# Interleaved banded groups in the second batch, with sums of v and half of the masks taken off the tensor engine, and 70 unread matmuls

## The chip, the core and the metric

The kernel runs on one core of a Trainium2 chip. The metric is device time in microseconds (us) of one execution. In the texts PE is the tensor engine (matmuls and transposes), DVE the vector engine, ACT the scalar engine, POOL the GpSimd engine and SP the engine that issues the DMAs.

## What is computed

The reference takes q, k and v of 8 batches x 8 heads x 576 tokens x 64 and sums two attentions per head: one on tokens that are averaged in fours (144 tokens, "pooled"), whose result is repeated four times, and one in which a token sees only the 7 tokens around it (the "band"). The result, as 4608 tokens x 512, goes through a layer that takes the maximum of three products, and then through an output product:

```python
pos = np.arange(S)
mask = np.abs(pos[:, None] - pos[None, :]) < factor
scores = scale * np.matmul(q, k.transpose(0, 1, 3, 2))
scores = np.where(mask, scores, -1000000000.0)
...
return (out_up + out_local).astype(np.float32)

def _moe_ref(x, w1, w2, w3, w_out) -> np.ndarray:
    h = np.maximum(np.maximum(x @ w1, x @ w2), x @ w3)
    return (h @ w_out).astype(np.float32)
```

In the program's inputs the weights are float64 (their 64 bits are read as two 32-bit words), and the products of the layer are made from a high and a low part of each operand: three matmuls (high x high, high x low, low x high) for each product.

## The kernel before

**Tiles and stages.** A batch has 512 tokens in 128 rows of four, and 64 tokens of tail; the tails of all batches make a ninth block. Half a batch (4 heads) is a group, n = 0 to 17; groups 2j and 2j+1 make batch j. For each batch `mlp_in` runs 216 matmuls of 128x512 (6 slices of the hidden layer x 3 weights x 4 slices of x x 3 parts) and `mlp_out` 72, so 2592 in nine blocks. `transposes(j, c)` adds the pooled result `od` to the band result `x` and splits the sum into `xhi` and `xlo` (ACT casts, DVE or POOL subtracts), which the layer's matmuls read.

**Two ways to do the band.** Groups 0 to 3 (`DENSE`) compute the band on PE: `band_load` loads, `band_transposes` (T) brings q and k to feature-major form, `band_scores` for each of two head pairs (A, B) makes 128x134 pieces of scores with an additive mask that a matmul `identr` x `maskr` writes to the PSUM bank first, then a maximum (DVE), an exponential (ACT) and a scaling (POOL or ACT). `band_values` (V, W) transposes the probabilities and multiplies them with v. Groups 4 to 17 do it on DVE, ACT and POOL (`scores`, `values`), with products of 128x1792 elements on DVE. The pooled attention is made by `tail_pooled` (t), `pooled_scores` (p), `band_pooled_values` (v: the sums of four rows of v, by matmuls of 128x256 with a matrix `sums` of zeros and ones) and `pooled_values` (o).

**Weights.** `weight_in` and `weight_out` turn 64-bit words into a float32 high and low part: an absolute value on ACT, a clamp (`tensor_scalar` with max and min, on DVE or POOL by `WENG`), three bit operations on DVE, a cast on ACT, a subtraction. In the profile the work tile is `wo` (`wa`), and the results are `whi` and `wlo`. The tags `whi2`, `whi3`, `whi4`, `whi5` (and `wlo`) serve groups 0 to 3 first as homes of scores and transposed q and k.

**What sets the order.** Nothing is issued as it is written. A `Recorder` takes down every operation with its tiles, then `place()` deals them to the engines by a list: each operation has a price per engine (`price`), a priority and the operations that it needs; the engine that is free first takes the ready operation with the lowest key (time, priority, order of writing). What may go to several engines goes to the one that ends first by these prices. A tile can be opened only when a buffer of its tag is free and it is among the next `WINDOW` tiles of its tag. The order of each engine is fixed by this before the program runs; on the chip an engine issues in that order and waits wherever an operand is not there. PE and the others are thus in order, and so is SP with the DMAs. PSUM has eight banks in two tags of four, `pm` and `pa`; the layer's matmuls use `pm`, the attention `pa`, and group 0 uses `pm` as well.

The first batch is written in the order of the string `ORDER`, groups 0 and 1 interleaved, at priority 0. The second batch is `block(1)`: `attention(2)` at priority 200, and after it `attention(3)` at 300. PE work has 2000 taken off its priority, and `mlp_in`, `mlp_out` stand at -100.

All instructions go through one line of `emit` (L374 in the profile), so the groups of the profile are told apart by their tiles.

```python
ORDER = "T0 T1 A0 A1 B0 V0 B1 V1 t0 p0 t1 p1 W0 W1 v0 o0 v1 o1"
PE_MASK = (0, 1, 2, 3)
WINDOW = {"pa": 4, "pm": 4}
```

## Time and profile before

| | |
|---|---|
| Median of 3 runs | 822.71 us (818.24 to 826.49) |
| The profiled execution's own time | 821.14 us |
| Its span | 819.4 us, 12160 instructions |
| Mean granted clock of PE | 0.975 |
| PE busy | 787.8 us (96%), 4064 matmuls |
| DVE busy | 660.5 us (81%) |
| ACT busy | 422.2 us (52%) |
| POOL busy | 361.6 us (44%) |
| Mean share of the DMA engines | 94 GB/s, 76.72 MB |

A row of the windows view gives a stretch in us from the span's start, its length, and then for each engine its busy time and its instructions, then the granted clock of PE as a share of the full one, the DMA share and GB/s. A row of the timeline gives start, duration, engine, line, operation, output and inputs, shapes and count, and in brackets the idle time ahead of it and what ended it. Matmuls overlap, so what one costs is read from the distance between two starts and not from its duration. A float32 matmul appears as two instructions in the profile, and as one in the order of the program; transposes, and matmuls of the rounded type (names that end in `r`), appear as one in both. The tile names are those of the tag: `xhi`, `whi`, `wo`, `pv`, `hh` carry several tenants in turn, so `whi<-pm,mxb` in the first 80 us is an exponential of scores.

### The profile page before, as it was taken

The page shows a single profiled execution, that of the slowest core. Times are in us where ns is not written, and L with a number is a line of the kernel's source. Part 1 is how long each engine was busy: PE and PEld are TensorE (multiplying, and loading weights), DVE is VectorE, ACT ScalarE, POOL GpSimd, SP SyncE. Part 2 cuts the span into 40 slices and gives each one's busy share as a digit, 9 for nine tenths or more (in the row PEclk, how much of TensorE's full clock was granted, in tenths as well). Part 3 has the DMA queues.
Part 4 walks back from the last instruction along what each step waited for, and adds up shares of the span by engine and source line. Part 5 has one row for each costly group of instructions (what it writes and reads, how often), then busy time and mean ns, then how long its engine had stood idle before and what let it go on. Part 6 is the DMA issues. An engine that isn't in the chain of part 4 may idle for free.

```text
span 819.4 us, 12160 instructions
## 1 busy us (share of the span) xinstructions
PE 787.8 (96%) x4064; PEld 609.9 (74%) x4064; DVE 660.5 (81%) x859; ACT 422.2 (52%) x1446; POOL 361.6 (44%) x522
## 2 busy tenths in 40 slices
PE   6879999999999999999899999999899999999997
PEld 4657776777777777777677777778677887888885
DVE  5999668799999999999999999999999962231220
ACT  7867657435583737567274746726483451121111
POOL 0642101136878847697477956768162341000000
PEclk9668999999999999999999999999999999999999
DMA  7754033334323423352234334422242210001002
GB/s 243 186 174 118 10 103 110 110 102 131 108 97 107 125 77 90 102 157 84 84 110 135 110 88 113 143 85 88 77 133 73 79 58 26 1 13 39 1 0 52
DMA packets 63177, 76.72 MB, mean 94 GB/s; under 512 B 21484, under 2 KB 43434, under 8 KB 63114
## 3 DMA queue, kind: packets, MB, share of 16 engines
q1 hardware_dynamic: 63114, 75.94, 30.8%
q8 instruction: 32, 0.52, 0.3%
q14 instruction: 31, 0.25, 0.1%
HBM read 66.49 MB, written 9.44 MB: 93 GB/s over the span
## 4 chain that ended last, share of the span: by engine, by line
PE 64%; DVE 20%; ACT 6%; issue 5%; DMA 2%; POOL 2%; POOLq 0%; SPq 0%; DVEq 0%; ACTq 0%
PE pm L374 52%; PE pa L374 11%; DVE prod L374 4%; DVE s L374 3%; DVE x L374 3%; ACT pv L374 2%; POOL pv L374 2%; DVE wo L374 1%; DMA v<-in_v_dram 1%; ACT wlo L374 1%; DVE y L374 1%; DVE pm L374 1%; DVE t L374 1%; DMA pv<-in_k_dram 1%; DVE xlo_0r L374 1%
## 5 line engine op out<-in xcount | busy, mean ns | idle before, releaser
L374 PE MATMUL pm<-xhi_0r,whi_0r 128*128 128x512 f32 x648 | 258.4, 399 | 0.0
L374 PE MATMUL pm<-xhi_0r,wlo_0r 128*128 128x512 f32 x648 | 258.3, 399 | 0.0
L374 PE MATMUL pm<-xlo_0r,whi_0r 128*128 128x512 f32 x648 | 258.2, 399 | 0.0
L374 POOL TENSOR_TENSOR pv<-v,s 128x256 f32<-128x256 f32 x247 | 177.6, 835 | 93.7 <-DVE s L374 72.1
L374 ACT ACTIVATE pv<-v,s 128x64 f32<-128x64 f32 x580 | 151.7, 412 | 21.8 <-DMA v<-in_v_dram 9.8
L374 PEld LDWEIGHTS pm<-xhi_0r,whi_0r 128*128 128x128 f32 x648 | 122.4, 189 | 28.3 <-issue 0.2
L374 PEld LDWEIGHTS pm<-xlo_0r,whi_0r 128*128 128x128 f32 x648 | 122.2, 189 | 28.1 <-issue 0.4
L374 PEld LDWEIGHTS pm<-xhi_0r,wlo_0r 128*128 128x128 f32 x648 | 122.1, 188 | 27.8
L374 DVE TENSOR_TENSOR prod<-k,q 128x1792 f32<-128x1792 f32 x56 | 119.2, 2128 | 1.1 <-DMA k<-in_k_dram 0.9
L374 DVE TENSOR_REDUCE x<-pv 128x256 f32<-128x1792 f32 x55 | 110.2, 2006 | 7.2 <-POOL pv L374 7.1
L374 DVE TENSOR_REDUCE s<-prod 128x28 f32<-128x1792 f32 x56 | 112.4, 2007 | 0.4
L374 DVE TENSOR_TENSOR t<-pm,t 128x512 f32<-128x512 f32 x54 | 36.9, 683 | 63.9 <-PE pm L374 63.8
L374 PE MATMUL pm<-wo_1r,hh_0r 128*128 128x512 f32 x216 | 85.6, 397 | 0.0
L374 PE MATMUL pm<-wo_1r,hh_1r 128*128 128x512 f32 x216 | 85.4, 399 | 0.0
L374 DVE TENSOR_TENSOR pm<-pm,t 128x512 f32<-128x512 f32 x54 | 37.3, 691 | 25.1 <-PE pm L374 24.9
L374 ACT CAST hh_1r<-pm 128x512 fp32r<-128x512 f32 x30 | 17.6, 588 | 71.3 <-DVE pm L374 71.3
L374 ACT COPY t<-pm 128x512 f32<-128x512 f32 x54 | 31.8, 589 | 40.0 <-PE pm L374 39.9
L374 ACT CAST hh_0r<-pm 128x512 fp32r<-128x512 f32 x24 | 14.1, 588 | 67.8 <-DVE pm L374 67.5
L374 PEld LDWEIGHTS pm<-wo_1r,hh_1r 128*128 128x128 f32 x216 | 41.0, 190 | 10.0 <-issue 0.5
L374 ACT COPY y<-pm 128x512 f32<-128x512 f32 x38 | 22.2, 588 | 49.6 <-PE pm L374 42.3
L374 PE MATMUL pm<-wo_0r,hh_1r 128*128 128x512 f32 x120 | 47.5, 400 | 0.1
L374 PEld LDWEIGHTS pm<-wo_1r,hh_0r 128*128 128x128 f32 x216 | 40.9, 189 | 9.1
(262 smaller groups left out, 1142.6 us busy)
## 6 DMA issues: line engine op xcount, KB each, us to landing
v<-in_v_dram SPq DMA_DIRECT2D x55, 320.0 KB
k<-in_k_dram SPq DMA_DIRECT2D x55, 320.0 KB
out_dram<-y SPq DMA_DIRECT2D x36, 256.0 KB
q<-in_q_dram SPq DMA_DIRECT2D x56, 128.0 KB
hh<-in_moe_w_dram SPq DMA_DIRECT2D x12, 512.0 KB
pv<-in_moe_w_dram SPq DMA_DIRECT2D x6, 512.0 KB
pv<-in_moe_w_out_dram SPq DMA_DIRECT2D x6, 512.0 KB
wo<-in_v_dram SPq DMA_DIRECT2D x12, 128.0 KB
```

The costliest lines, as they stand in the source:

```text
L374: getattr(self.engines[o.eng], method)(*map(real, args), **{k: real(x) for k, x in kw.items()})
```

## The change

1. **Second batch interleaved.** `second_block` takes the place of `block(1)`: groups 2 and 3 are written in the order of a new string `ORDER2`, both at priority 200, through the same table of steps (`steps_of`) as the first batch. Group 3 gets the separate buffers that group 1 had (`OTHER = (1, 3)`), so the two groups don't share them.
2. **Masks.** `PE_MASK` goes from four groups to groups 0 and 1. In groups 2 and 3 the 16 mask matmuls go; DVE adds the mask to each bank of scores and writes the sum to SBUF (`sm`), where the maximum and the exponential read it.
3. **Sums of v.** `band_pooled_values` no longer uses matmuls: for each head it loads 128x256 of v once more, and DVE or POOL add the halves (128x128 per head), then the halves of the halves (128x256 per group). The matrix `sums`, its load and its tile go.
4. **Unread matmuls.** `WARM` goes from 0 to 70: 70 matmuls `identr` x `identr` of 128x512 into one `pm` bank that nobody reads, at priority 1e6, so that `place()` puts one wherever PE has nothing else ready by its reckoning.
5. **Transposes of groups 0 and 1** write their output with a step of four elements into the PSUM bank (`inorder`), so that the copy out of it reads and writes in a row. Before, PE wrote in a row and ACT read with a step.
6. **Loads of the tails** of k and v in groups 0 and 1 use the two buffers of tag `q` in place of the one of `traw`.
7. **Prices and windows.** `place()` reckons a `tensor_scalar` on POOL with 4.1 ns an element in place of 2.2, and `WINDOW` is 3 in place of 4 for both PSUM tags. `GATE` is empty and does nothing.

```diff
-WARM = 0
+WARM = 70
-PE_MASK = (0, 1, 2, 3)
+PE_MASK = (0, 1)
+OTHER = (1, 3)
+ORDER2 = "L2 T2 L3 A2 B2 V2 W2 T3 t2 p2 A3 B3 v2 o2 V3 W3 t3 p3 v3 o3"
-WINDOW = {"pa": 4, "pm": 4}
+WINDOW = {"pa": 3, "pm": 3}
...
+            if method == "tensor_scalar":
+                return 140.0 + 4.1 * n, True
             return 140.0 + (1.68 if kw.get("op") == ALU.mult else 2.2) * n, True
...
-            raw = new([N64, FAC * D], tag="traw", name=f"traw_{n}_{g}")
+            raw = new([N64, FAC * D], tag="q", bufs=2, name=f"traw_{n}_{g}") if n < 2 and g else new([N64, FAC * D], tag="traw", name=f"traw_{n}_{g}")
...
+                    inorder = ps.rearrange("p (r f) -> p f r", f=FAC)
                     for f in range(FAC):
-                        pe.transpose(ps[:, P * f : P * f + P], byf[:, f], ident)
-                    to, fr = dst.rearrange("p (r f) -> p f r", f=FAC), ps.rearrange("p (f r) -> p f r", f=FAC)
+                        pe.transpose(inorder[:, f], byf[:, f], ident)
+                    to, fr = dst, ps
...
-            for i in range(2):
+            for i in range(2) if on_pe else ():
                 pe.matmul(sps[i], identr, rest, start=True, stop=False, skip_group_check=True)
-                banks[tp, i] = sps[i]
...
+            for i in range(2):
+                banks[tp, i] = sps[i]
+                if not on_pe:
+                    dve.tensor_tensor(out=sm[:, i, 2 * tp : 2 * tp + 2], in0=sps[i], in1=rest.bitcast(F32), op=ALU.add)
+                    banks[tp, i] = sm[:, i, 2 * tp : 2 * tp + 2]
...
-        ps = bank([P, HH, D], tag, f"psv_{n}")
-        for u in range(FAC):
-            pe.matmul(ps, sums[:, 96 - 32 * u : 96 - 32 * u + P], vt[:, u], start=u == 0, stop=False, skip_group_check=True)
-        pe.matmul(ps[96:], sums[:6, 64:96], vb[1][:, 1], start=False, stop=True, tile_position=(0, 96), skip_group_check=True)
-        copy(vd, ps)
+        hv = new([P, HH, 2 * D], tag="hv", name=f"hv_{n}")
+        vd = state[n]["vd"] = new([P, HH, D], tag="vd", bufs=2, name=f"vd_{n}")
+        for g in range(HH):
+            vv = new([P, FAC * D], tag="v", bufs=2, name=f"v_{n}_{g}")
+            sp.dma_start(vv, row_tokens(v, j, h0 + g, 0, FAC * D))
+            halves(n, "v", vv, hv[:, g], BENG)
+        tt(vd, hv[:, :, :D], hv[:, :, D:], ALU.add, BENG)
...
+    def second_block():
+        open_block(1)
+        if 3 in DENSE:
+            steps_of(ORDER2, ("pa", "pa"))
...
     turn(0)
-    block(1)
+    with at(200.0, LAG):
+        second_block()
```

How the order of the instructions moves is shown at three places. The first is the start of PE's order. `pm_104`, `pm_111` are PSUM banks, `xhi` and `xlo` hold q and k of groups 0 and 1 in the order that the transposes want, `identr` is the operand of the unread matmuls. Before:

```order
L374 MATMUL pm_104<-ident_65,xhi_0_99 128x128 x4
L374 MATMUL pm_111<-ident_65,xhi_0_101 128x128 x4
L374 MATMUL pm_120<-ident_65,qd_85 128x3 x2
L374 MATMUL pm_126<-ident_65,xlo_0_113 128x128 x4
L374 MATMUL pm_104<-ident_65,xlo_0_115 128x128 x4
```

And now:

```order
L378 MATMUL pm_94<-identr_0r 128x512 x11
L378 MATMUL pm_116<-ident_65,xhi_0_106 128x128 x4
L378 MATMUL pm_127<-ident_65,xhi_0_108 128x128 x4
L378 MATMUL pm_94<-identr_0r 128x512 x3
L378 MATMUL pm_138<-ident_65,xlo_0_123 128x128 x4
L378 MATMUL pm_116<-ident_65,xlo_0_125 128x128 x4
L378 MATMUL pm_127<-ident_65,qd_85 128x3 x2
L378 MATMUL pm_94<-identr_0r 128x512 x3
```

Eleven unread matmuls stand ahead of the first transpose, and three behind each of the next pairs. The other 50 stand further down, the last four ahead of the pooled values of group 0; none stands behind the first matmul of the layer.

The second place is where the layer begins on PE, in the middle of group 2: `xhi`, `xlo` with `whi`, `wlo` are matmuls of the layer, `maskr` with `identr` a mask, `whi_0_73` holds q and k of group 2, and `pv` its untransposed q and k. Before:

```order
L374 MATMUL pa_149<-ident_65,qd_85 128x3 x2
L374 MATMUL pa_176<-maskr_0r,identr_0r 128x268
L374 MATMUL pm_104<-xhi_0r,whi_0r 128x512
L374 MATMUL pm_104<-xhi_0r,wlo_0r 128x512
L374 MATMUL pa_166<-maskr_0r,identr_0r 128x268
L374 MATMUL pm_104<-xlo_0r,whi_0r 128x512
L374 MATMUL pa_157<-maskr_0r,identr_0r 128x268
L374 MATMUL pa_176<-whi_0_73 128x134
L374 MATMUL pa_157<-whi_0_73 128x134
```

And now:

```order
L378 MATMUL pm_138<-xhi_0r,whi_0r 128x512
L378 MATMUL pa_165<-ident_65,qd_85 128x3 x2
L378 MATMUL pm_138<-xhi_0r,wlo_0r 128x512
L378 MATMUL pa_174<-ident_65,pv_83 128x128 x4
L378 MATMUL pm_138<-xlo_0r,whi_0r 128x512
L378 MATMUL pm_138<-xhi_0r,whi_0r 128x512
L378 MATMUL pm_138<-xhi_0r,wlo_0r 128x512
L378 MATMUL pm_138<-xlo_0r,whi_0r 128x512
L378 MATMUL pa_203<-whi_0_73 128x134
L378 MATMUL pa_195<-whi_0_73 128x134
```

The masks are gone and the score matmuls stand alone between those of the layer. Further down the transposes of group 3 stand behind 54 matmuls of the layer where they stood behind 60, and the last pooled values of group 3 behind 165 where they stood behind 147.

The third place is on DVE, ahead of the first split of x. `wo` is the work tile of the weights (TENSOR_SCALAR is a clamp or the bit operation with a shift, SCALAR_TENSOR_TENSOR one of the other two bit operations), `od` the pooled result, `xlo` the low part of x. Before:

```order
L374 SCALAR_TENSOR_TENSOR wo_225<-hh_87,wo_225 128x512
L374 TENSOR_TENSOR x_454<-x_454,od_720 128x512
L374 TENSOR_TENSOR x_656<-x_656,od_720 128x512
L374 TENSOR_TENSOR tq_231<-th_209 64x128
L374 SCALAR_TENSOR_TENSOR wo_225<-hh_87,wo_225 128x512
L374 TENSOR_SCALAR wo_225<-wo_225 128x512
L374 TENSOR_TENSOR th_209<-traw_171 64x128
L374 TENSOR_SCALAR wo_225<-wo_225 128x512
L374 TENSOR_TENSOR xlo_0r<-x_454,xhi_0r 128x512
L374 TENSOR_TENSOR xlo_0r<-x_656,xhi_0r 128x512
```

And now:

```order
L378 TENSOR_TENSOR hv_273<-v_211 128x128
L378 TENSOR_SCALAR wo_286<-wo_286 128x512 x2
L378 TENSOR_TENSOR tq_242<-th_228 64x128
L378 SCALAR_TENSOR_TENSOR wo_286<-hh_87,wo_286 128x512 x2
L378 TENSOR_SCALAR wo_286<-wo_286 128x512 x2
L378 SCALAR_TENSOR_TENSOR wo_286<-hh_87,wo_286 128x512 x2
L378 TENSOR_SCALAR wo_286<-wo_286 128x512 x2
L378 TENSOR_TENSOR x_510<-x_510,od_822 128x512
L378 TENSOR_TENSOR x_803<-x_803,od_822 128x512
L378 TENSOR_TENSOR wlo_0r<-wo_286,whi_0r 128x512 x2
L378 SCALAR_TENSOR_TENSOR wo_286<-hh_87,wo_286 128x512
L378 TENSOR_TENSOR xlo_0r<-x_510,xhi_0r 128x512
```

More of the weights' work stands ahead of the first split of x: counted over DVE's order up to that row, 24 operations of TENSOR_SCALAR on `wo` in place of 16, 23 of SCALAR_TENSOR_TENSOR in place of 20, 7 additions of halves of v (`hv`) and 2 of the second halves (`vd`) in place of none, and four copies of 128x512 out of PSUM fewer. POOL's order has no TENSOR_SCALAR on `wo` any more, where it had seven.

More of the change, by code (lines that the diff above doesn't have):

```diff
@@ L155, in add @@
         o.seq = len(self.ops)
-        o.need, o.tiles = set(), []
+        o.need, o.tiles = set() if "SP" in forms else set(self.behind), []
         pe = "PE" in forms
@@ L432, in local_global_attention_maxout_kernel @@
     KW = SEG + 6
-    sums = new([P, 96 + P], tag="sums", name="sums")
     KB = 2 * FAC * (P + 6)
@@ L580, in pooled_scores @@
         act.mul(nm, nm, scale)
-        pd = own(n, 1).rearrange("p (a b x) -> p a b x", a=2, b=2) if n == 1 else new([P, 2, 2, SD], tag="pd", name=f"pd_{n}")
+        pd = own(n, 1).rearrange("p (a b x) -> p a b x", a=2, b=2) if n in OTHER else new([P, 2, 2, SD], tag="pd", name=f"pd_{n}")
         pdt = new([N64, SD], tag="pdt", name=f"pdt_{n}")
@@ L737, in band_transposes @@
         q4, k4, kh = st["q4"], st["k4"], st["kh"]
-        qkT = st["qkT"] = own(n, 0).rearrange("p (a b x) -> p a b x", a=2, b=2) if n == 1 else new([P, 2, 2, SD], tag="qkT", name=f"qkT_{n}")
+        qkT = st["qkT"] = own(n, 0).rearrange("p (a b x) -> p a b x", a=2, b=2) if n in OTHER else new([P, 2, 2, SD], tag="qkT", name=f"qkT_{n}")
         for pr in range(2):
@@ L785, in band_scores @@
                     pp = slice(64 * i, 64 * i + 64)
-                    pe.matmul(sps[i][:, u], qT[pp, t0 : t0 + P], kT[pp, t0 : t0 + P + 6], start=False, stop=u == 1, skip_group_check=True)
+                    pe.matmul(sps[i][:, u], qT[pp, t0 : t0 + P], kT[pp, t0 : t0 + P + 6], start=not on_pe, stop=not on_pe or u == 1, skip_group_check=True)
+            for i in range(2):
[3 more added lines that the diff above has]
+                    banks[tp, i] = sm[:, i, 2 * tp : 2 * tp + 2]
         mx = new([P, 2, FAC], tag="mxb", bufs=2, name=f"mxb_{n}_{pr}")
@@ L945, in turn, with steps_of @@
                 transposes(j, c)
+    mark = {}
+    def steps_of(order, tags):
+        steps = {
+            "L": band_load,
+            "T": lambda n: band_transposes(n, tags[n % 2]),
+            "A": lambda n: band_scores(n, 0, tags[n % 2]),
+            "B": lambda n: band_scores(n, 1, tags[n % 2]),
+            "t": tail_pooled,
+            "p": lambda n: pooled_scores(n, tags[n % 2]),
+            "V": lambda n: band_values(n, 0, tags[n % 2]),
+            "W": lambda n: band_values(n, 1, tags[n % 2]),
+            "v": band_pooled_values,
+            "o": lambda n: pooled_values(n, tags[n % 2]),
+        }
+        for step in order.split():
+            steps[step[0]](int(step[1]))
+            mark[step] = rec.ops[-1]
     def first_block():
         open_block(0)
-        tags = ("pm", "pa")
         load_constants()
-        for n in range(2):
-            band_load(n)
+        steps_of("L0 L1", ("pm", "pa"))
         load_rest()
@@ L956, in first_block @@
                 keep_busy(WARM, "warm0")
-        steps = {
-            "T": lambda n: band_transposes(n, tags[n]),
-            "A": lambda n: band_scores(n, 0, tags[n]),
-            "B": lambda n: band_scores(n, 1, tags[n]),
-            "t": tail_pooled,
-            "p": lambda n: pooled_scores(n, tags[n]),
-            "V": lambda n: band_values(n, 0, tags[n]),
-            "W": lambda n: band_values(n, 1, tags[n]),
-            "v": lambda n: band_pooled_values(n, tags[n]),
-            "o": lambda n: pooled_values(n, tags[n]),
-        }
-        for step in ORDER.split():
-            steps[step[0]](int(step[1]))
+        steps_of(ORDER, ("pm", "pa"))
+    def second_block():
+        open_block(1)
+        if 3 in DENSE:
+            steps_of(ORDER2, ("pa", "pa"))
+        else:
+            steps_of("L2 T2 A2 B2 V2 t2 p2 W2 v2 o2", ("pa", "pa"))
+            attention(3)
     with at(0.0, LAG):
```

38 lines of the change are left out of this document (12 added, 26 removed).

## The prediction

> **What bounds the kernel now.** I first cut the span into stages with the windows view. The columns are the stretch, its length, then PE, PEld, DVE, ACT and POOL busy with their instructions, the granted clock, DMA share and GB/s:
>
> ```profile
> 0.00:9.50 9.50, 3.15 (x15) 2.80 (x16) 1.79 (x13) 4.39 (x6) 0.20 (x4) 1.00 0.76 238
> 9.50:30.00 20.50, 16.55 (x110) 12.37 (x109) 18.51 (x52) 18.18 (x65) 7.55 (x7) 0.79 0.74 218
> 30.00:73.00 43.00, 37.50 (x308) 26.69 (x307) 40.73 (x90) 31.65 (x105) 16.97 (x10) 0.74 0.58 159
> 73.00:150.00 77.00, 75.65 (x534) 55.83 (x534) 55.61 (x130) 48.36 (x171) 10.03 (x15) 1.00 0.27 78
> 150.00:680.00 530.00, 521.54 (x2530) 404.65 (x2528) 515.47 (x538) 298.43 (x1068) 326.84 (x487) 0.99 0.34 103
> 680.00:813.70 133.70, 133.37 (x575) 107.59 (x575) 28.39 (x42) 20.56 (x35) 0.00 (x0) 1.00 0.05 16
> 813.70:819.40 5.70, 0.00 (x0) 0.00 (x0) 0.00 (x0) 0.59 (x1) 0.00 (x0) 0.76 0.19 46
> ```
>
> Up to 73 us PE has gaps (57.2 of 73 us busy) and a clock of three quarters, while DVE is busy for 59.2 of the 63.5 us from 9.5 on. From 73 to 813.7 PE idles for 1.35 + 8.46 + 0.33 = 10.1 us only; then 5.7 us of output follow. The chain of waits says the same of the end:
>
> ```profile
> 47.85 4.88 PE pm L374 x14
> ...
> 680.92 132.73 PE pm L374 x571
> ```
>
> For the last 133 us PE works off matmuls that wait for nobody, so DVE, 97% busy from 150 to 680, could be late there without cost. So the time is the point at which the layer's matmuls begin, plus PE's work after it, plus PE's 10 us of waits, plus the output. What one matmul costs is the distance between starts, here in PE's timeline where the layer begins:
>
> ```profile
> 73.08 0.39 PE L374 MATMUL pm<-xhi_0r,whi_0r 128*128 128x512 f32 x1
> 73.31 0.39 PE L374 MATMUL pm<-xhi_0r,wlo_0r 128*128 128x512 f32 x1
> 73.54 0.29 PE L374 MATMUL pa<-maskr_0r,identr_0r 128*128 128x268 f32 x1
> 73.66 0.39 PE L374 MATMUL pm<-xlo_0r,whi_0r 128*128 128x512 f32 x1
> ...
> 78.48 0.40 PE L374 MATMUL pa<-maskr_0r,identr_0r 128*128 128x268 f32 x1
> 78.81 0.72 PE L374 MATMUL pa<-wlo 64*128 64x134 f32 x4
> ```
>
> One matmul of the layer takes 0.23 us, a mask 0.12 us between two of the layer and 0.33 us between score matmuls.
>
> **Work that leaves PE behind 73 us.** The busy time of the mask matmuls in the second batch, and of the matmuls with `sums` up to 73 us and after, by the windows view of these tiles:
>
> ```profile
> 73.00:150.00 77.00, 4.99 (x16) 2.84 (x16) 0.00 (x0) 1.00 0.27 78
> ...
> 0.00:73.00 73.00, 7.48 (x20) 4.88 (x20) 0.79 0.65 186
> 73.00:150.00 77.00, 5.08 (x20) 3.14 (x20) 1.00 0.27 78
> ```
>
> All of this second part is on the path, since PE is busy around it. The sums give 5.1 us. The masks lie between 16 x 0.12 = 1.9 and 4.99 us; they stand about equally in both surroundings, so I take 3.5. Together −8.6 us. In their place DVE gets 16 additions of 128x268; the nearest row is the 128x256 addition of 418 ns below, so 16 x 0.42 = 6.7 us, which DVE's 77 − 55.6 = 21.4 idle us between 73 and 150 hide. If that cover were gone, it would be late with group 4, and that costs nothing until the second batch's x is late: the split of that x is issued at 169 us, PE begins with it at 186:
>
> ```profile
> 169.16 2.49 DVE xlo_0r L374 x4
> ...
> 185.72 0.39 PE L374 MATMUL pm<-xhi_0r,whi_0r 128*128 128x512 f32 x1
> ```
>
> That is 186 − 172 = 14 us of slack, and groups 2 and 3, now interleaved, should end earlier on DVE rather than later.
>
> **The start.** What DVE and POOL do there has these rows (groups of the first 76 us; the POOL row from its first 130 us; count, busy us, mean ns of one):
>
> ```profile
> L374 DVE SCALAR_TENSOR_TENSOR wo<-hh,wo 128x512 uint32<-128x512 uint32 x20 | 14.6, 728 | 0.4
> L374 DVE TENSOR_SCALAR wo<-wo 128x512 f32<-128x512 f32 x5 | 2.1, 415 | 0.0
> L374 DVE TENSOR_TENSOR hd<-whi 128x256 f32<-128x256 f32 x6 | 2.5, 418 | 0.6 <-ACT whi L374 0.5
> L374 DVE TENSOR_TENSOR qkT<-hd 128x128 f32<-128x128 f32 x6 | 1.8, 292 | 0.2
> L374 DVE COPY y<-pm 128x512 f32<-128x512 f32 x2 | 1.3, 664 | 0.0
> L374 POOL TENSOR_SCALAR wo<-wo 128x512 f32<-128x512 f32 x7 | 15.6, 2237 | 20.3 <-ACT wo L374 20.3
> ```
>
> The new price takes the clamp from POOL, where it does cost 2.24 us, and gives it to DVE at 0.42. Ahead of the first split of x, DVE's order has 8 more TENSOR_SCALAR on `wo` (3.3 us), 3 more SCALAR_TENSOR_TENSOR (2.2), 7 half-sums of v at 0.29 (2.0) and 2 second sums at 0.42 (0.8): +8.3 us. It has four copies of 128x512 and the one of the sums fewer: 4 x 0.66 + 0.42 = −3.1. The rest, small operations, about cancels. So +5.2 us, on an engine that is full there. Against it stands an earlier beginning. Two rows of ACT show a copy out of PSUM with a step, and one in a row; two of PE and one of ACT the first transposes and when the unread matmuls could begin:
>
> ```profile
> 12.07 1.11 ACT L374 ACTIVATE whi<-pa 128x512 f32<-128x512 f32 x1
> 71.44 0.60 ACT L374 ACTIVATE whi<-pa 128x512 f32<-128x512 f32 x1
> ...
> 2.54 0.30 ACT L374 CAST identr_0r<-ident 128x128 fp32r<-128x128 f32 x1 [0.53 <-DMA ident<-in_ident_dram]
> 6.35 1.97 PE L374 MATMUL pm<-ident,xhi 128*128 128x128 f32 x8 [6.35 <-DVE xhi L374]
> 70.74 1.97 PE L374 MATMUL pa<-ident,pv 128*128 128x128 f32 x16
> ```
>
> Eight copies become about 0.5 us shorter each, 4 us of ACT. But the 11 unread matmuls begin at 2.84 and, at the cold step of 0.43 us (below), end at 7.6, 1.2 us after the first transposes could have begun. Of the 4 us some 1.5 may reach DVE, whose idle time lies in its first 9.5 us (7.7 us) and not behind them (2.0 us up to 30). The transposes themselves write with a step now. No row of this trace shows PE writing so. Their price lies between nothing, as the read gains what the write loses nowhere, and a doubling: 32 x 0.12 = 3.9 us; below nothing is excluded, since they move the same elements. I take nothing, because PE has its gaps there. The Trainium skill ("PSUM — Partial Sum Buffer", Specifications) says that PSUM is reached in lines of 8 bytes and that any access that isn't contiguous slows matmuls significantly; by that, the upper end holds, spread over eight banks, and about half of it would delay the start.
>
> So DVE reaches the split of x 5.2 − 1.5 = 3.7 us later:
>
> ```profile
> 68.13 1.29 DVE L374 TENSOR_TENSOR xlo_0r<-x,xhi_0r 128x512 fp32r<-128x512 f32 x2
> 71.88 1.28 DVE L374 TENSOR_TENSOR x<-x,od 128x512 f32<-128x512 f32 x2
> ```
>
> The first two splits end at 69.4 + 3.7 = 73.1, still in time for the matmul that read them at 73.66. The other two sums come 3.7 us later than 71.9, and PE, which was given their matmuls within 3 us, can put the scores of group 2 ahead but not all of the 3.7: I take +2 us. Here DVE is what counts: the 7.5 us of sums that leave PE ahead of 73 us bring nothing, as the split doesn't wait for PE.
>
> **The 70 unread matmuls** end ahead of the layer. At 0.23 us they take 16.3 us; PE had 73 − 57.2 = 15.8 us without work there, and loses 7.5 us of sums, so they fit. The clock is what they can change. In the stretch after small matmuls at 150 us it shows as steps of the layer's matmuls:
>
> ```profile
> 150.90 0.66 PE L374 MATMUL pm<-xhi_0r,wlo_0r 128*128 128x512 f32 x1
> 151.35 0.63 PE L374 MATMUL pm<-xlo_0r,whi_0r 128*128 128x512 f32 x1
> ...
> 154.34 0.47 PE L374 MATMUL pm<-xhi_0r,whi_0r 128*128 128x512 f32 x1
> 154.65 0.39 PE L374 MATMUL pm<-xhi_0r,wlo_0r 128*128 128x512 f32 x1
> ```
>
> 0.43 us a step for 3.4 us, then 0.23. So dense matmuls bring the full clock within 3.4 us. The Trainium skill ("TensorE: Matmul & The Clock Gate", Part 1) gives the same: about 3.4 us of work lift the clock from half to full, and an idle window of that length drops it again; this trace agrees with 3.4 us. A full clock in place of 0.74 shortens PE's small matmuls ahead of 73 us, which again lie beside DVE's work. The interleaved order should spare the slow spell at 150 us, half of 3.4 = 1.7 us; of this I take 1.
>
> **The sum.** −5.1 (sums) − 3.5 (masks) + 2 (late x) − 1 (slow spell) = −7.6 us against the execution's own 821.1 us (span 819.4 and 1.7 around it). The waits of PE behind 73 us I leave at 10 us: the order is new everywhere, so each can go or come. The median is 822.7, 1.6 above that execution, so 822.7 − 7.6 = 815.
>
> **Rivals.**
>
> *The start is PE's.* The chain of waits runs through PE for much of 47 to 73 us, with sums in it (the 4.88 us at 47.85). If that, not DVE, decides, the start shortens by the 7.5 us of sums and by some of the slow clock (0.74 over 43 us means some 22 us at half). With DVE's 3.7 us against it, I put it at 6 to 9 us earlier: 815 − 2 − 7 = 806. For it speaks the chain, against it DVE's 40.7 of 43 us. Chance 0.2.
>
> *Waits take it back.* PE's new order sets steps of groups 4 to 17 earlier among the layer's matmuls than DVE delivers. The 8.5 us of such waits double: 815 + 8 = 823. For it: DVE is 97% busy there. Against: it gains from its idle 21 us. Chance 0.14.
>
> *The second batch starves PE as the first did.* Written like the first, it could give the first's picture: from 9.5 to 73 us PE was idle for 9.5 of 63.5 us, and its clock at three quarters. Waits of 9.5 us and a quarter of 77 us at half clock, 9.6 us, make 815 + 19 = 834. It decides from 16 us of waits on. Against it: 165 matmuls of the layer stand between those steps, none did in the first. Chance 0.1.
>
> *The unread matmuls stay cold.* At 0.43 us all 70 take 30.1 us, 57.2 − 7.5 + 30.1 + 2.8 = 82.6: the layer begins 9.6 us later, and 815 + 9.6 − 2 = 823. The steps at 150 us speak against it. Chance 0.06.
>
> **The numbers.** The forecast, 815 us, has 0.5, with 810 to 821 for the bounds of the masks (±1.6), the late x (0 to 4) and some waits. I call 1% the smallest difference that such a measurement tells from none: 814.5 and 831. Faster: 0.45 of the forecast's chance with the whole first rival, 0.25 + 0.2 = 0.45. Same: the rest of the forecast, 0.25, with 0.18 of the two that land at 823: 0.43. Slower: the third rival and the tail of the others, 0.12. The range for 8 in 10 is 803 to 826.
>
> **What would show it.** Right: the matmul `xhi,whi` begins between 70 and 75 us with DVE full ahead of it; the second batch has no `maskr` and no `sums` matmul and is some 8 us of PE shorter; POOL has no clamp and the start's clock is near 1.0; PE's waits behind the start are 6 to 14 us. Wrong: a start of the layer under 68 us (the first rival), PE idle by over 5 us between the start and the second batch's end (the third), or unread matmuls with 0.43 us steps throughout.

## The result, and the profile after

The changed kernel takes 818.41 us (median of 20 runs, 810.59 to 821.78), the kernel before 822.45 us (20 runs beside them). The ratio is 0.9946, with a 95% interval from 0.9924 to 0.9967: faster by 4.0 us, about half of the 7.6 us forecast, and by the bound of 1% no change. The profiled execution of the changed kernel took 817.85 us, with a span of 816.1 us. Runs that took over 1.5% longer than the fastest of the same kernel are left out of its median and ratio, here and below.

The windows of the changed kernel, by the stages used before (stretch, its length, then PE, PEld, DVE, ACT and POOL busy with their instructions, granted clock, DMA share, GB/s):

```profile
0.00:9.50 9.50, 6.53 (x24) 5.33 (x25) 1.72 (x12) 3.91 (x6) 0.20 (x4) 1.00 0.76 236
9.50:30.00 20.50, 19.34 (x127) 14.87 (x126) 19.41 (x54) 15.63 (x61) 6.68 (x9) 1.00 0.72 217
30.00:73.00 43.00, 40.25 (x337) 29.64 (x335) 42.24 (x95) 35.12 (x116) 11.33 (x12) 0.88 0.67 185
73.00:150.00 77.00, 73.10 (x523) 54.35 (x522) 68.66 (x161) 51.35 (x173) 13.58 (x20) 1.00 0.36 110
150.00:680.00 530.00, 519.81 (x2514) 405.40 (x2513) 497.96 (x516) 291.39 (x1041) 338.54 (x499) 0.98 0.33 101
680.00:810.00 130.00, 130.00 (x563) 105.30 (x561) 27.47 (x40) 20.20 (x35) 0.00 (x0) 1.00 0.05 14
```

The start has its clock now (1.00 and 0.88 where 0.79 and 0.74 stood). From 73 to 150 us DVE has 13 us more to do, which its idle time takes. But PE idles for 3.9 us there instead of 1.35, and from 150 to 680 us for 10.2 us instead of 8.46, at a clock of 0.98 instead of 0.99. The chain of waits ends as before, in a run of PE's matmuls that wait for nobody:

```profile
667.82 142.51 PE pm L378 x615
```

PE's timeline where the layer begins:

```profile
68.89 1.02 PE L378 MATMUL pa<-ident,pv 128*128 128x128 f32 x4 [1.09 <-ACT x L378]
69.56 0.78 PE L378 MATMUL pm<-xhi_0r,whi_0r 128*128 128x512 f32 x1
70.27 0.37 PE L378 MATMUL pa<-ident,qd 3*128 3x3 f32 x2
70.57 0.80 PE L378 MATMUL pm<-xhi_0r,wlo_0r 128*128 128x512 f32 x1
71.16 1.06 PE L378 MATMUL pa<-ident,pv 128*128 128x128 f32 x4
71.87 0.74 PE L378 MATMUL pm<-xlo_0r,whi_0r 128*128 128x512 f32 x1
```

It begins at 69.56 us, 3.5 us earlier than before (73.08). So the time can be told as a sum again: where the layer begins, PE's work from there to its last matmul, PE's idle time in between, and what the half clock costs in between (half of its duration). The first two terms of the next rows are the stretch from the layer's first matmul to the end of PE's last one; the kernel before first, then the changed one:

```profile
73.08:813.64 740.56, 730.48 (x3636) 567.99 (x3635) 599.39 (x708) 367.26 (x1273) 336.87 (x502) 1.00 0.28 85
```

```profile
69.56:810.32 740.76, 726.67 (x3608) 567.59 (x3606) 597.53 (x719) 364.87 (x1253) 355.33 (x522) 0.99 0.28 87
```

Idle time is length less PE busy: 10.1 and 14.1 us. The half clock, by the granted clock in the trace, which goes in steps of 3.4 us, holds for 6.8 us of that stretch before (two spells, at 151 and 581 us) and for 19.9 us after (at 69, 318, 380 and 578 us). What is left is PE's work at the full clock:

| term (us) | before | after | difference |
|---|---|---|---|
| start of the layer | 73.1 | 69.6 | −3.5 |
| PE's work behind it | 727.1 | 716.7 | −10.4 |
| PE's idle time behind it | 10.1 | 14.1 | +4.0 |
| half of the half-clock time behind it | 3.4 | 10.0 | +6.6 |
| end of the last matmul | 813.6 | 810.3 | −3.3 |

So the work did leave PE, and as much came back as waits and as slow clock. The 3.3 us that are left are about what the layer starts earlier. The first three waits behind the start (total, times, longest), out of PE's waits:

```profile
PE pa L378 <- POOL vd L378: 2.7, 1, 2.7
PE pa L378 <- DVE xlo_0r L378: 2.5, 1, 2.5
PE pa L378 <- DVE ptl L378: 2.0, 1, 2.0
```

Within half a microsecond of the end of each of the three, a half-clock spell begins. The one at 577 us in PE's timeline:

```profile
574.45 0.39 PE L378 MATMUL pm<-wo_1r,hh_1r 128*128 128x512 f32 x1
577.36 1.92 PE L378 MATMUL pa<-qkT 64*128 64x144 f32 x8 [2.52 <-DVE xlo_0r L378]
...
579.84 0.80 PE L378 MATMUL pm<-wo_0r,hh_0r 128*128 128x512 f32 x1
580.43 0.63 PE L378 MATMUL pm<-wo_1r,hh_0r 128*128 128x512 f32 x1
580.86 0.63 PE L378 MATMUL pm<-wo_1r,hh_1r 128*128 128x512 f32 x1
...
584.59 0.40 PE L378 MATMUL pm<-wo_1r,hh_1r 128*128 128x512 f32 x1
584.83 0.40 PE L378 MATMUL pm<-wo_0r,hh_0r 128*128 128x512 f32 x1
```

Ahead of the wait and from 584.6 us on the layer's matmuls start 0.23 us apart, in between 0.43. The wait cost 2.5 us, and the spell behind it half of 6.8 us more; that the one brought the other is taken up in the last section. The runs without a profile fit this: of the changed kernel's 20 runs, the four with a granted clock of 0.991 or more took 810.6 to 814.1 us, the three at 0.981 or less that came behind the profiled one 819.4 to 821.4.

### The profile page after: what moved, and what is told of

Same layout as the page of the kernel before. It is cut to its first block, busy times and chain, and to the rows that moved or that the text cites. A ratio compares the mean times of both kernels' runs of the same rounds, so it can differ in the third digit from the quotient of the medians.

```text
span 816.1 us, 12243 instructions
## 1 busy us (share of the span) xinstructions
PE 789.3 (97%) x4078; PEld 614.9 (75%) x4078; DVE 657.5 (81%) x874; ACT 418.2 (51%) x1430; POOL 370.3 (45%) x543
## 4 chain that ended last, share of the span: by engine, by line
PE 68%; DVE 18%; POOL 4%; ACT 3%; DMA 3%; issue 2%; SPq 0%; DVEq 0%; ACTq 0%; POOLq 0%
PE pm L378 57%; PE pa L378 10%; DVE s L378 4%; POOL pv L378 4%; DVE prod L378 3%; DVE wo L378 2%; DVE x L378 1%; DMA hh<-in_k_dram 1%; DVE xlo_0r L378 1%; DMA pv<-in_moe_w_dram 1%; ACT pv L378 1%; DVE wlo_0r L378 1%; DVE mxb L378 1%; DVE t L378 1%; DVE hd L378 1%
## 5 line engine op out<-in xcount | busy, mean ns | idle before, releaser
L378 POOL TENSOR_TENSOR pv<-v,s 128x256 f32<-128x256 f32 x255 | 187.4, 851 | 100.0 <-DVE s L378 83.3
L378 ACT ACTIVATE pv<-v,s 128x64 f32<-128x64 f32 x548 | 143.4, 411 | 16.6 <-DMA v<-in_v_dram 7.6
L378 POOL TENSOR_TENSOR th<-traw 64x128 f32<-64x128 f32 x42 | 26.9, 640 | 57.9 <-DVE x L378 18.1
L378 ACT CAST hh_1r<-pm 128x512 fp32r<-128x512 f32 x30 | 17.7, 589 | 67.3 <-DVE pm L378 67.0
L378 ACT CAST hh_0r<-pm 128x512 fp32r<-128x512 f32 x24 | 14.1, 587 | 71.3 <-DVE pm L378 71.2
```

Source lines behind the costliest of these rows:

```text
L378: getattr(self.engines[o.eng], method)(*map(real, args), **{k: real(x) for k, x in kw.items()})
```

## The experiments

The table has the sum's terms from each profile, and the ratio of the runs to those of the kernel before, with its interval. "Half" is the half-clock time behind the start; the work is the stretch less the idle time and half of that.

| kernel | start | work | idle | half | ratio to before |
|---|---|---|---|---|---|
| before | 73.1 | 727.1 | 10.1 | 6.8 | 1 |
| changed | 69.6 | 716.7 | 14.1 | 19.9 | 0.9946 [0.9924, 0.9967] |
| PE spared 9.1 us | 69.6 | 707.2 | 14.0 | 10.2 | 0.9824 [0.9796, 0.9853] |
| DVE's reduces cut by 12 us | 69.3 | 717.3 | 17.6 | 13.7 | 0.9898 [0.9868, 0.9928] |
| not interleaved | 70.2 | 716.4 | 25.5 | 30.7 | 1.0147 [1.0124, 1.0171] |
| masks back on PE | 69.5 | 721.8 | 17.8 | 34.1 | 1.0061 [1.0029, 1.0094] |
| sums back on PE | 71.2 | 724.6 | 9.9 | 17.1 | 0.9946 [0.9926, 0.9967] |
| masks and sums back | | | | | 1.0182 [1.0141, 1.0223] |
| no unread matmuls | 75.8 | 716.5 | 14.8 | 12.1 | 0.9932 [0.9906, 0.9958] |
| before + unread matmuls | 74.3 | 729.9 | 10.8 | 10.2 | 1.0046 [1.0015, 1.0076] |
| no unread, sums back | 69.2 | 726.6 | 8.8 | 17.1 | 1.0013 [0.9990, 1.0036] |
| PE planned later | 69.6 | 717.6 | 20.6 | 6.8 | 0.9954 [0.9926, 0.9981] |
| old price on POOL | 67.5 | 719.5 | 17.7 | 10.2 | 0.9962 [0.9939, 0.9985] |
| transposes in order | 69.8 | 718.2 | 13.9 | 10.2 | 0.9916 [0.9884, 0.9948] |

The work is steady: the seven kernels whose matmuls behind the start are those of the changed kernel lie between 716.4 and 719.5 us, the kernel before and the one that only adds unread matmuls to it at 727.1 and 729.9. So a term of the work is good to about 3 us. An earlier start and the work behind it also trade with each other: 36 matmuls left PE's second batch, but the changed kernel has only 28 fewer behind the start, as some that stood ahead of it now stand behind (four of group 2's transposes, at 71.16 us, are among them). What differs from kernel to kernel is idle time and half-clock time. Each profile is one execution, so such a row explains its own span, and the ratio is the verdict.

My first theory was that the changed kernel's waits come from PE running ahead of DVE, and that later planned PE steps, or work given back to PE, would lower them.

### PE planned later

```diff
-        o.lag = self.lag
+        o.lag = self.lag + 4000.0 if "PE" in forms and self.late else self.lag
```

`late` holds for the groups that are not banded; the planner then takes it that PE's steps there get their inputs 4 us later than it otherwise reckons.

> The changed kernel, with one edit: from group 4 on the planner reckons 4 us more until PE may use a result of another engine, so PE's attention steps stand later among the layer's matmuls; no work is added or taken. Theory (what PE was spared behind the start is eaten by PE's waits, 14 us against 10 before, and by the half-clock spells that follow them, some 20 us of spells against 7 before): waits behind the start fall under 8 us, spells under 10 us, time 4 to 9 us under the changed kernel's 818.4, so 809 to 814. Rival (the waits only stand where other engines would have made PE wait anyway, DVE being 94% busy): the waits move elsewhere, time within 2 us of 818.4.

817.89 us: no change, so the rival holds. PE's idle time rose to 20.6 us, where my theory had less than 8, and its half-clock time fell to 6.8. Idle time and half of the half-clock time are 24.0 us together, and 24.1 in the changed kernel: the planner's view of PE moves the loss about and doesn't lower it.

### Without the unread matmuls

```diff
-WARM = 70
+WARM = 0
```

> The changed kernel without the 70 unread matmuls (WARM = 0). Theory (the start hangs on DVE's order, and the unread matmuls lie in PE's gaps): the layer's first matmul moves by less than 2 us from 69.6, the time by less than 3 us from 818.4, and the clock ahead of 73 us falls to some 0.75. Rival (the full clock is what brought the 3.5 us at the start): the first matmul comes at 72 to 74 us and the time is 3 to 5 us longer, 821 to 823.

815.38 us, not worse than the changed kernel. Windows of the start:

```profile
9.50:30.00 20.50, 16.72 (x102) 12.20 (x101) 15.75 (x49) 13.53 (x63) 7.03 (x10) 0.75 0.65 199
30.00:73.00 43.00, 40.51 (x281) 28.86 (x280) 36.63 (x89) 31.94 (x104) 7.47 (x7) 0.50 0.64 175
```

The layer's first matmul in PE's timeline:

```profile
75.84 0.80 PE L378 MATMUL pm<-xhi_0r,whi_0r 128*128 128x512 f32 x1
```

Without them PE runs at the half clock throughout the 43 us ahead of the layer, and in this profile the layer begins 6.3 us later. So the theory was wrong about the start, and the rival about the time: PE lost 3.2 us less to waits and slow clock behind the start here (14.8 + 6.0 us), and the median is 3 us lower, with intervals that overlap.

### Masks back on PE, sums back on PE

```diff
-PE_MASK = (0, 1)
+PE_MASK = (0, 1, 2, 3)
```

> The changed kernel with the 16 mask matmuls of groups 2 and 3 back on PE and off DVE. Theory (every us of PE work behind the start is on the path): PE is busy some 3.5 us longer between 70 and 150 us and the time is 2 to 5 us longer, 820.5 to 823. Rival (in the second batch PE now waits for DVE, and the mask additions on DVE cost as much as the matmuls): no change or up to 2 us shorter, 816.5 to 818.5.

1.0061, some 9.5 us more than the changed kernel (0.0115 of 822), where 2 to 5 were expected for the price on PE. The price is 5.1 us in the table, good to 3 us. The rest should lie in waits and half-clock time, 17.8 and 34.1 us in its profile; but that execution took 833.8 us, 5 us above the median, so these two say little of the others. Its longest wait, with the half-clock steps behind it, in PE's timeline:

```profile
239.29 0.42 PE L378 MATMUL pa<-ident,ptl 128*64 128x128 f32 x1 [4.66 <-DVE ptl L378]
...
240.48 0.63 PE L378 MATMUL pm<-xlo_0r,whi_0r 128*128 128x512 f32 x1
240.91 0.63 PE L378 MATMUL pm<-xhi_0r,whi_0r 128*128 128x512 f32 x1
```

It lies 40 us behind the second batch, in a group that the masks don't touch.

The other part alone:

```diff
+        ps = bank([P, HH, D], tag, f"psv_{n}")
+        for u in range(FAC):
+            pe.matmul(ps, sums[:, 96 - 32 * u : 96 - 32 * u + P], vt[:, u], start=u == 0, stop=False, skip_group_check=True)
+        pe.matmul(ps[96:], sums[:6, 64:96], vb[1][:, 1], start=False, stop=True, tile_position=(0, 96), skip_group_check=True)
+        copy(vd, ps)
...
-            sp.dma_start(vv, row_tokens(v, j, h0 + g, 0, FAC * D))
-            halves(n, "v", vv, hv[:, g], BENG)
```

> The changed kernel with the sums of v of groups 0 to 3 back as matmuls on PE, without the extra loads of v and the additions on DVE and POOL. Theory: 5 us of PE work come back behind the start; at the start 9 half-sums and sums (2.8 us) leave DVE, and the layer's first matmul stays within 2 us of 69.6; time 3 to 6 us longer, 821 to 824. Rival (the sums ahead of 73 us stood in the chain of the start, so that taking them off PE made the 3.5 us there): the first matmul comes at 73 us or later and the time is 7 to 10 us longer, 825 to 828.

817.76 us, no change, against +3 to +6 expected: my theory falls here. PE's work did rise, by 7.9 us in the table; the sums alone are busy for 5.0 us behind the start by the windows of their tile, where 5.1 was forecast:

```profile
71.17:200.00 128.83, 4.97 (x20) 3.20 (x20) 0.96 0.33 100
```

The idle time fell by 4.2 us, to 9.9, and half of the half-clock time by 1.4. DVE was spared too: 591.1 us busy behind the start, 6.4 less than in the changed kernel, with the halves of v no longer its work. This profile is of the longest of six runs, 3.9 us above their median, so its terms add up to more than the runs show.

### Which engine is the bound

Work taken off PE that brings nothing could mean that PE is not the bound. So on each of the two full engines some work was left out by itself. On PE, one of the twelve matmuls of every third product in the first seven blocks was left out:

```diff
+                if j < B - 1 and i == 2:
+                    del ops[10]
```

> The changed kernel with 42 matmuls of the layer left out (one of the twelve of every third product, in the first seven blocks of tokens, so between about 73 and 640 us; the output is then not the reference's): 42 x 0.216 us = 9.1 us less PE work, nothing taken from another engine. Both theories start from the changed kernel's 818.4 us. Theory 'two full engines': between 200 and 600 us DVE is 94 to 99 of 100 us busy in every profile so far, so PE, spared, only waits longer for DVE's results, and the waits bring half-clock spells: 814 to 820 us, PE's idle time behind the start up from 14 us by 5 or more. Rival 'PE alone is the bound': what PE is spared is gained: 808 to 811 us, idle time as before.

On DVE, half of one reduce in four was left out in the groups that are not banded:

```diff
+            wide = D // 2 if g == 3 and j < B else D
-            dve.tensor_reduce(out=s[:, g], in_=prod.rearrange("p o (f d) -> p o f d", d=D), axis=AX.X, op=ALU.add)
+            dve.tensor_reduce(out=s[:, g], in_=prod.rearrange("p o (f d) -> p o f d", d=D)[..., :wide], axis=AX.X, op=ALU.add)
```

> The changed kernel with half of one reduce in four left out on DVE (the sum of the products of q and k over 32 of the 64 numbers, one head of each of the 12 groups that are not banded; the output is then not the reference's): 12 x about 1.0 us (half of the 2.007 us that one takes) = 12 us less DVE work, PE's work untouched. Theory 'two full engines': DVE stands further ahead of PE, the waits for its results and the half-clock spells that follow them shrink: 807 to 814 us, PE idle behind the start 5 to 10 us instead of 14. Rival 'PE alone is the bound, its waits are accidents of the order': 816 to 820 us, idle time 12 us or more. If this one gains and the run with fewer matmuls gains too, both engines are bounds at once, and neither theory alone holds.

PE spared 9.1 us: 806.72 us, 0.9824, so 0.0122 × 822 = 10 us less than the changed kernel, or 6 to 14 by the ends of the two intervals. That is the rival, and a little beyond its 808 us: PE is the bound, and what it is spared without a price elsewhere is gained whole. Its work fell by 9.5 us and its idle time stayed:

```profile
69.64:796.02 726.38, 712.34 (x3567) 555.69 (x3565) 601.72 (x721) 365.38 (x1254) 349.46 (x520) 0.99 0.29 89
```

DVE's reduces cut by 12 us: 0.9898, a median of 813.58 us and some 4 us less, inside the 807 to 814 of the theory of two full engines; the intervals of this kernel and the changed one touch. But the theory's mechanism doesn't show. PE's idle time is 17.6 us, where 5 to 10 were asked for, in a profile of the longest of the six runs. And the edit didn't spare DVE 12 us. The window from the layer's first matmul to the end of the last one:

```profile
69.34:811.00 741.66, 724.10 (x3609) 564.37 (x3607) 593.92 (x728) 364.65 (x1255) 340.80 (x515) 0.99 0.28 87
```

DVE is busy for 3.6 us less than in the changed kernel, and POOL for 14.5 us less. The reduces do take 11.3 us less of DVE, but other rows take more: the additions of halves of v (`hv`) are 20 rows with 10.2 us there and 19 rows with 18.6 us here. So this run gives no price for a microsecond of DVE. Nor does the sums' result come out as a sum of prices: with the sums back, PE has 5 to 8 us more to do, DVE 6.4 us less, and the time is the same. That the two cancel is what was measured; by which path DVE's share counts stays open.

### The order and the work together

Interleaving undone, the rest kept:

```diff
-            steps_of(ORDER2, ("pa", "pa"))
+            steps_of("L2 T2 A2 B2 V2 t2 p2 W2 v2 o2", ("pa", "pa"))
+            with at(300.0, LAG):
+                steps_of("L3 T3 A3 B3 V3 t3 p3 W3 v3 o3", ("pa", "pa"))
```

> The changed kernel with the two banded groups of the second batch written one behind the other again, group 2 at priority 200 and group 3 at 300; everything else as changed. Theory: interleaving moves no work and PE's waits come from DVE's load, so the time is within 3 us of the changed kernel: 815.5 to 821.5 us. Rival 'the interleaved groups cause the new waits' (the one of 2.7 us for the values of a pooled group at 316 us and the one of 2.0 us at 377 us): 811 to 815 us. Rival 'interleaving is what pays for the change': 822 us or more.

834.46 us: 16 us slower than the changed kernel and 12 slower than the one before, as the second rival had it (822 or more). The windows of the second batch in this kernel, then in the changed one:

```profile
73.00:150.00 77.00, 68.79 (x442) 50.86 (x439) 62.00 (x147) 42.58 (x149) 12.79 (x16) 0.91 0.31 93
150.00:200.00 50.00, 43.63 (x214) 33.05 (x215) 45.37 (x57) 16.78 (x35) 12.33 (x16) 0.93 0.30 99
```

```profile
150.00:200.00 50.00, 48.38 (x220) 37.87 (x219) 49.55 (x58) 21.30 (x64) 24.51 (x32) 1.00 0.35 110
```

From 73 to 200 us PE idles for 8.2 + 6.4 = 14.6 us, against 3.9 + 1.6 in the changed kernel, and the clock falls to 0.91 and 0.93. Three of these waits in PE's timeline, two among group 3's steps and one in the layer:

```profile
132.91 1.58 PE L378 MATMUL pa<-ident,whi 128*128 128x128 f32 x8 [1.29 <-ACT whi L378]
137.76 0.69 PE L378 MATMUL pa<-y,wo 128*64 128x128 f32 x2 [3.26 <-DVE y L378]
...
187.37 0.50 PE L378 MATMUL pm<-wo_1r,hh_1r 128*128 128x512 f32 x1 [3.10 <-ACT wo_1r L378]
```

DVE is not full there (62.0 of 77 us). By 131.2 us PE has done 144 matmuls of the layer, four of its six slices, and the next begins at 143.86. In between it has only group 3's steps, whose results come round over DVE and ACT, and waits for them. So this is the third rival of the prediction, second batch starved like the first, at the 834 us that the prediction put on it; interleaving is what keeps it away.

The opposite, interleaved with masks and sums on PE:

```diff
-PE_MASK = (0, 1)
+PE_MASK = (0, 1, 2, 3)
+            pe.matmul(ps, sums[:, 96 - 32 * u : 96 - 32 * u + P], vt[:, u], start=u == 0, stop=False, skip_group_check=True)
```

> The changed kernel with the masks of the second batch and the sums of v back on PE: of the change there stay the interleaved order of the second batch, the 70 unread matmuls and the small edits. Theory 'the parts complete each other' (interleaving only fills the waits that a longer chain over DVE leaves, which with masks and sums on PE are not there): 826 to 833 us, as the masks back alone (830.2 us) and the sums back alone (817.8 us) add up to; PE's idle time between the layer's start and 200 us no more than 4 us. Rival 'interleaving pays by itself': 816 to 822 us, as its removal alone cost 16 us. PE's work behind the start is 9 to 13 us above the changed kernel's by either.

1.0182, a median of 837.8 us and beyond both expectations; the nearer one is that the parts complete each other. Its profiled execution took 1085 us, so its terms are left out of the table and where its time goes isn't shown. With the unread matmuls in all four, the ratios to the kernel before are:

| | masks, sums on PE | off PE |
|---|---|---|
| one group behind the other | 1.0046 (without the small edits) | 1.0147 |
| interleaved | 1.0182 | 0.9946 |

Either part alone costs 8 to 11 us, both together save 8. A sum with one term for each part can't hold this. The first corner is the weak one, as it lacks the small edits: for the two parts to add up, it would have to be 1.038 with them, and that kernel wasn't tried.

### The unread matmuls alone, and with the sums

```diff
-WARM = 0
+WARM = 70
```

> The kernel before with the 70 unread matmuls alone (822.1 to 822.5 us without them). Theory: they keep the clock up in the start, where the kernel before shows three half-clock spells, 30.7 us together, and so bring the layer's first matmul from 73.1 us to 68 to 70 us; but the waits behind it grow by as much, as the changed kernel without them has shown (layer's first matmul 6.3 us later, same time): 820 to 824 us. Rival 'an earlier layer is an earlier end': 817 to 819 us. Rival 'the unread matmuls stand in the way': first matmul of the layer not earlier than 73 us, 823 to 826 us.

This is the kernel before with that one edit. 1.0046, slower by 1 to 6 us; the layer's first matmul came at 74.34 us, not earlier, so the last rival holds, though the median, 827.8 us, lies above its 826. The unread matmuls didn't keep the clock up where the layer begins: PE had half the clock from 60.5 to 70.7 us.

The changed kernel without them and with the sums on PE:

> The changed kernel without the two parts whose removal cost nothing: no unread matmuls (815.4 us alone) and the sums of v back on PE (817.8 us alone). If both add up: 813 to 817 us, the fastest kernel of this study. If one stood in for the other (the unread matmuls keep the clock up for the sums' matmuls ahead of the layer): layer's first matmul at 77 us or later, 818 to 824 us.

1.0013, a median of 822.6 us: the two removals don't add up, though the layer began at 69.23 us, so neither expectation holds whole. Its profile has 17.1 us at half clock, 8.8 us of idle time and 10 us more work on PE than the changed kernel's. With the sums on PE, then, taking the unread matmuls out costs 5.5 us (1.0013 against 0.9946, 2 to 9 us by the ends of the intervals), where with the sums off PE it cost nothing. Why is open: the layer began earlier without them.

### Two small edits

The planner's price for a clamp on POOL, 2.2 ns an element again:

```diff
-                return 140.0 + 4.1 * n, True
+                return 140.0 + 2.2 * n, True
```

> The changed kernel with the planner's old price for tensor_scalar on POOL (2.2 ns an element instead of 4.1): the planner gives some of the weights' clamps to POOL again, where one takes 2.24 us, instead of 0.42 us on DVE. Theory 'small edits matter little': DVE is spared 1 to 3 us by 73 us, POOL holds 5 to 15 us more, the layer starts within 2 us of 69.6 us and the time is 816 to 822 us. Rival 'the price brought the earlier start' (69.6 us instead of 73.1 us): layer's start 72 us or later, 821 to 826 us.

818.25 us, no change; the layer began at 67.47 us, 2 us earlier than in the changed kernel.

The transposes of the first batch written in a row, and read with a step:

```diff
-                        pe.transpose(inorder[:, f], byf[:, f], ident)
-                    to, fr = dst, ps
+                        pe.transpose(ps[:, P * f : P * f + P], byf[:, f], ident)
+                    to, fr = dst.rearrange("p (r f) -> p f r", f=FAC), ps.rearrange("p (f r) -> p f r", f=FAC)
```

> The changed kernel with the transposes of the first batch written without a step, and the step back in the copies that read them. In the changed kernel's trace eight transposes written with a step take 1.03 us at the full clock, 0.13 us each, as transposes without a step do, and the copies behind them got shorter. Theory: the step costs PE nothing and spares ACT and DVE 4 us within the first 30 us, of which the layer's start sees 0 to 2 us: undone, 818 to 821 us. Rival 'the step is the reason of the earlier start': layer's start 72 us or later, 821 to 825 us. Rival 'the step slows the transposes': 814 to 817 us.

0.9916, a median of 814.1 us, lower than the changed kernel with intervals that overlap: nearest to the last rival, but not by slower transposes. The gain isn't sure, either: over all of its twelve runs, which spread from 810.3 to 824.9 us, the median is 819.1. The groups of PE's instructions from 5 to 15 us, with a step (changed kernel) and then in a row:

```profile
L378 PE MATMUL pm<-ident,xhi 128*128 128x128 f32 x8 | 1.0, 272 | 0.0
```

```profile
L378 PE MATMUL pm<-ident,xhi 128*128 128x128 f32 x8 | 1.0, 272 | 0.0
```

They take the same to the nanosecond. What moved the 4 us, if it is no chance, stays open: the two profiles differ by 9.7 us of half-clock time, and the wait that ends at 577 us is missing here, with its spell.

No kernel that computes the whole beat the changed one beyond the intervals.

## Why the time fell inside the forecast's range, and half of its steps failed

**What leaves PE** (−8.6 forecast): right, as far as a term good to 3 us can tell. PE's work behind the start fell by 10.4 us. The sums measured 5.0 us busy (5.1), the masks 5.1 by the work of the kernel that has them back; that is near the upper bound (4.99), but doesn't rule out the 3.5 taken from the middle. The cover held: the 16 additions of the mask take DVE 6.2 us (6.7), it took up 13 us in all between 73 and 150 us, and stood at 68.7 of 77 us.

**The start** (+2 for a late x): wrong in sign. DVE did reach x later, by 1.8 and 1.4 us at the two rows that the prediction counted from (68.13 and 71.88 us before), though not by 3.7:

```profile
69.95 1.66 DVE L378 TENSOR_TENSOR xlo_0r<-x,xhi_0r 128x512 fp32r<-128x512 f32 x2
73.25 1.28 DVE L378 TENSOR_TENSOR x<-x,od 128x512 f32<-128x512 f32 x2
```

The step that failed is "Here DVE is what counts". In the kernel before, the first half of x was there when ACT had cast it, at 68.6 us. PE had no gap ahead of the layer, and came to it 4.5 us later, with sums among its matmuls. The row of ACT, then PE's:

```profile
67.47 1.14 ACT L374 CAST xhi_0r<-x 128x512 fp32r<-128x512 f32 x2
```

```profile
61.65 1.06 PE L374 MATMUL pa<-ident,wlo 128*128 128x128 f32 x4
...
63.58 3.04 PE L374 MATMUL pa<-wo,sums 128*128 128x256 f32 x8
66.55 0.61 PE L374 MATMUL pa<-k,sums 6*32 6x256 f32 x2
...
72.64 0.28 PE L374 MATMUL pa<-ident,qd 3*128 3x3 f32 x2
```

In the changed kernel the same casts end at 68.35 us, no earlier to speak of, and the layer begins 1.2 us behind them:

```profile
67.13 1.22 ACT L378 CAST xhi_0r<-x 128x512 fp32r<-128x512 f32 x2 [0.78 <-DVE x L378]
```

So it was PE that came earlier, as the first rival had it, by 3.5 us and not by its 6 to 9 (69.56 us lies just under the 70 to 75 named as right, and over the 68 named as that rival's sign). I read the chain's 4.88 us of PE as a reason for that rival and weighed it less than DVE's busy share. What PE was spared is less clear. The sums alone aren't it: with them back the layer began at 71.2 and 69.2 us. Neither are interleaving (70.2 without), the masks (69.5), POOL's price (67.5) or the transposes (69.8), each undone by itself. Without the unread matmuls it began at 75.8 us, the only edit whose removal brings a late start back; yet without them and with the sums it began at 69.2. What goes with the start in all 13 profiles is the clock of PE in the last 15 us ahead of the layer. Where half the clock held for 6.8 us of them or more (kernel before, before + unread, no unread matmuls), PE began 5.0, 5.2 and 9.6 us behind the end of the first cast of x; where it held for 1.5 us or less (the other ten), 0.4 to 3.3 us. This was read from the profiles and no run set the clock by itself. The prediction had put a full clock at nothing there, since PE's small matmuls "lie beside DVE's work". The late second half of x did cost a wait, 1.2 us.

**The waits, left at 10 us**: 14.1, at the upper edge of the 6 to 14 named, and half of what the rival "waits take it back" held. Of these, 5.5 us lie between the layer's start and 200 us (1.4 before). That is over the 5 us which the prediction named as the sign of its third rival, but that rival's time did not come; the kernel that isn't interleaved shows what it looks like. **The slow spell spared** (−1): wrong in sign, and the largest miss. The spell at 151 us did go, but there are four where there were two, and their half is 10.0 us instead of 3.4. The forecast gave waits no second price, though the profile of before had one such case, a wait of 3.5 us that ends at 579 us with a spell behind it at 581:

```profile
579.46 1.35 PE L374 MATMUL pa<-qkT 64*128 64x144 f32 x8 [3.51 <-DVE xlo_0r L374]
```

The Trainium skill ("TensorE: Matmul & The Clock Gate", Part 1), which I had cited, sets the fall of the clock at an idle window of about 3.4 us; no wait of the changed kernel behind its start is that long, and with each of three waits of 2.0 to 2.7 us a spell came. The measurement decides.

**The unread matmuls**: they did what was said (a clock of 1.00 and 0.88 from 9.5 to 73 us, none behind the layer's start; the first eleven still ran 0.43 us apart). In the changed kernel that is worth nothing in the time, as forecast, though the layer begins 6.3 us earlier with them. It isn't so everywhere: they cost 1 to 6 us in the kernel before, and gain 5.5 with the sums on PE. **Transposes with a step** at nothing: right for PE, to the nanosecond. The Trainium skill ("PSUM — Partial Sum Buffer", Specifications) has any access that isn't contiguous slow matmuls significantly; these transposes didn't slow.

**What the sum could not hold.** Interleaving had no term but the spared spell. It is worth 16 us as long as masks and sums are off PE, and by the table of four it costs 11 when they are on it. Against the forecast's terms the start came out 5.5 us better and the work 1.8, the waits 4.0 us worse and the clock 7.6: −7.6 became −3.3 in the profiles by four errors, two of each sign. So it is luck as much as reckoning that 818.4 lies within 810 to 821. By the prediction's bound of 1% the change is none (0.43), not faster (0.45). (70 x 0.23 is 16.1 us and not the prediction's 16.3; nothing hangs on it.)

## What to carry to other kernels

In an order that is written out for in-order engines, an edit that moves work between engines and one that moves the order are not two terms: cost them as one, by looking where the bound engine will have nothing it may do. A bound engine can pay for a wait twice when its clock follows its load: ask for each wait of two microseconds or more what the steps behind it cost. To price a full engine, leave a known amount of work out of it and time that; but read in the profile how much the engine was spared in all, since here 11 us less of reduces became 3.6 us less of DVE's time.

## What was not expected of the hardware

In 13 profiles there are 28 waits of PE of 1.9 to 4.7 us behind the layer's start. With 23 of them went a half-clock spell of 3.4, 6.8 or, once, 13.7 us, which began during the wait, within about 3 us of its end or, once, just ahead of it; of 41 waits between 1.0 and 1.9 us, 11 had one. The length alone doesn't decide. The kernel before, at 391 us, waits longer than the changed kernel at 379 us, for the same tile, and keeps its clock. Before:

```profile
391.35 0.30 PE L374 MATMUL pa<-ident,ptl 128*64 128x128 f32 x1 [2.25 <-DVE ptl L374]
...
391.75 0.50 PE L374 MATMUL pm<-xhi_0r,whi_0r 128*128 128x512 f32 x1
392.09 0.40 PE L374 MATMUL pm<-xhi_0r,wlo_0r 128*128 128x512 f32 x1
```

After:

```profile
379.24 0.30 PE L378 MATMUL pa<-ident,ptl 128*64 128x128 f32 x1 [1.98 <-DVE ptl L378]
...
379.64 0.79 PE L378 MATMUL pm<-xhi_0r,wlo_0r 128*128 128x512 f32 x1
380.23 0.63 PE L378 MATMUL pm<-xlo_0r,whi_0r 128*128 128x512 f32 x1
```

The spells come in whole steps of 3.4 us, and all changes of the clock in one profile lie on one grid of such steps. Where a wait lies on that grid tells more than its length. In the 13 profiles 2759 steps behind the layer's start have the full clock. In 18 of them PE was idle for 57% of the step or more, and every one was followed by a step at half clock; of 49 with 30 to 57%, 13 were, and of the 2692 with less, 5. The wait of the changed kernel lies in one step, and is 58% of it. That of the kernel before is spread over two, and the fuller has 39%. So some 2 us without work were enough where they fell into one step. The Trainium skill (the same Part 1) says that the window runs freely, and the grid agrees with that. Idle time and grid were read from the traces, where the ends of matmuls are modelled; no run put a wait at a chosen place, so the link is seen in many cases and not tested by an edit.
